# Expert weights split in blocks of 640 columns, their tails multiplied in half modes, squares set apart

## The chip, the cores and the metric

The kernel runs on one core of one Trainium2 chip. The metric is the device time of one execution in microseconds; the time of a kernel is the median of its runs. TensorE (PE in the profile) does the matmuls, VectorE (DVE) and GpSimd (POOL) element-wise work, ScalarE (ACT) copies and activations, SyncE (SP) issues DMAs.

## The reference

Three layers follow each other on 3072 tokens of width 320: a recurrent attention with gates (mLSTM), a mixture of eight experts of which each token goes to one, and a gated layer.

```python
x = attention(q, k, v, gates).reshape(3072, 320)
expert_idx = np.argmax(normed(x) @ normed(expert_emb).T / tau, axis=1)
for e in range(8):
    mask = expert_idx == e
    h = np.maximum(x[mask] @ w1[e], 0.0)             # w1[e]: 320 x 1024
    out[mask] = gate_w[mask, None] * (h @ w2[e])     # w2[e]: 1024 x 320
gate = 1.0 / (1.0 + np.exp(-(out @ w_gate)))         # 320 x 1536
y = (gate * (out @ w_val)) @ w_out                   # 1536 x 320
```

The products are wanted in float32. The kernel makes each from three in half precision: an operand is split in a high half (a copy to float16) and a low half (the operand minus its copy), and high × high, high × low and low × high are added up.

## The kernel before

TensorE goes through three stages: attention up to 131 us, the experts from 131 to 336 us, the gated layer from 336 to 698 us.

**Expert stage.** Tokens are sorted by expert and stand in columns. There are nine runs: runs 0 and 1 are the 512 tokens of expert 0 in two windows of 256 columns, runs 2 to 8 are experts 1 to 7 with windows of 512, 480, 448, 416, 384, 352 and 336 columns. `expert_run(n)` (L1123) does a run in eight steps f, one for each 128 of the 1024 hidden units. In a step `l1_tile` (L1035) makes the hidden values in a PSUM bank `h_ps`, `hidden` (L1136) turns them into `hh` on ScalarE (L1138) and `hl` on VectorE (L1139), and `expert_l2` (L1050) multiplies the hidden values of two steps earlier into the three output banks `y_ps`. The model width 320 is 128 + 128 + 64. For the two slices of 128 each layer has three products per f. For the tail of 64, layer one has a stacked weight tile `w1s` that holds the high half on 64 rows and the low half on the other 64, and layer two has the last 128 columns of `w2h`, high and low half side by side; both then need two full products. So a step has 8 + 8 products of w columns and a run 128. The tails are scaled by 2 to the KT and KU, which is undone later. At the end of a run the tokens of the next are transposed (`transpose_part`, L1021) from rows `xrow` into `xh` and `xl`; a last block that is not full is transposed in as many rows as it has.

**Splits of the weights.** An expert's weights come in four pieces p for each layer, two f's a piece, into raw tiles `w1raw` and `w2raw` with two slots each (p modulo 2), by SyncE. `split_w1` and `split_w2` (L234, L250) split a piece by two ScalarE copies (tail and main part), a small VectorE subtraction for the tail (L216) and a GpSimd subtraction of 512 columns for the main part (L247, L261). `expert_steps` (L1453) sets by hand at which step f of which run a piece is split: odd f's take layer two, even ones layer one, and the load of the piece two further on follows in the same step. In the same steps VectorE works on blocks of the later weights, which arrive as raw 64-bit words: `f64_split` (L1194) is a chain of bit operations on tiles `fa` and `fb` (L1202 to L1219). Each engine runs its instructions in the order in which this code emits them.

**Gated stage.** It has 72 steps t, six groups of 512 tokens by twelve f's. `gated_a` and `gated_b` make gate and value products, in pairs of 64 rows that use both halves of the array; ScalarE takes the sigmoid (L1847) and the copy to `hh` (L1860), and tiny ScalarE copies `seen` (L1817) tell TensorE that the other half's products are done before a bank's rows are swapped. From t = 24 on the loop takes two entries of the list `checks` after each step's `gated_h`; among them are sums of squares of the output weights (`sqw`, L1752) on ScalarE.

## Time and profile before

| | us |
|---|---|
| median of three runs | 704.57 |
| lowest and highest run | 704.1 and 707.03 |
| profiled execution | 709.01 |
| its span | 707.0 |
| attention in it, up to | 131.02 |
| expert runs in it | 131.02 to 336.17 |
| gated stage in it | 336.17 to 697.6 |

The profile shows one execution. TensorE's row of products has the start and the length of each; since products overlap in the array, the distance of two starts, and not the length, is what one costs. The row `PEld` is the loading of weights, which goes beside the products. In the waits an engine's idle time is put down to the instruction that ended it.

### The profile page before, as it was taken

The page shows a single profiled execution, that of the slowest core. Times are in us where ns is not written, and L with a number is a line of the kernel's source. Part 1 is how long each engine was busy: PE and PEld are TensorE (multiplying, and loading weights), DVE is VectorE, ACT ScalarE, POOL GpSimd, SP SyncE. Part 2 cuts the span into 40 slices and gives each one's busy share as a digit, 9 for nine tenths or more (in the row PEclk, how much of TensorE's full clock was granted, in tenths as well). Part 3 has the DMA queues.
Part 4 walks back from the last instruction along what each step waited for, and adds up shares of the span by engine and source line. Part 5 has one row for each costly group of instructions (what it writes and reads, how often), then busy time and mean ns, then how long its engine had stood idle before and what let it go on. Part 6 is the DMA issues. An engine that isn't in the chain of part 4 may idle for free. (4 is left out here: it accounts for less than half of the span.)

```text
span 707.0 us, 17947 instructions
## 1 busy us (share of the span) xinstructions
PE 681.2 (96%) x6955; PEld 428.1 (61%) x6955; DVE 424.8 (60%) x928; ACT 419.7 (59%) x1063; POOL 328.1 (46%) x392
## 2 busy tenths in 40 slices
PE   6999999999999999999999999999999999999994
PEld 6899998885445556666555555545544555555552
DVE  7978888797789999887898873343211122211111
ACT  5887886866966677778665554455455453333332
POOL 8968888543754766674010005343243324324222
PEclk9999999999999999999999999999999999999998
DMA  7655875555445566651223211010010001001001
GB/s 231 212 190 180 276 223 160 150 170 162 138 149 177 162 197 191 197 163 57 57 84 88 63 57 40 1 39 1 2 38 2 1 2 38 2 2 39 1 2 41
DMA packets 39865, 70.47 MB, mean 100 GB/s; under 512 B 4818, under 2 KB 28460, under 8 KB 39772
## 3 DMA queue, kind: packets, MB, share of 16 engines
q1 hardware_dynamic: 36764, 59.61, 28.2%
q0 software_dynamic: 3008, 9.64, 4.2%
q8 instruction: 56, 0.92, 0.6%
q14 instruction: 37, 0.30, 0.2%
HBM read 60.55 MB, written 8.68 MB: 98 GB/s over the span
## 5 line engine op out<-in xcount | busy, mean ns | idle before, releaser
L1848 DVE SCALAR_TENSOR_TENSOR sgm<-v_ps,sgm 128x512 f32<-128x512 f32 (+1 forms) x74 | 49.9, 676 | 201.8 <-ACT sgm L1847 201.8
L1861 POOL TENSOR_TENSOR hl<-sgm,hh 128x512 f16<-128x512 f32 x54 | 62.4, 1159 | 214.2 <-ACT hh L1860 214.1
L1803 PE MATMUL v_ps<-xg,wvh 64*128 64x512 f16 x290 | 108.8, 375 | 3.9 <-ACT seen L1817 3.8
L1803 PE MATMUL g_ps<-xg,wgh 64*128 64x512 f16 x290 | 108.8, 375 | 0.0
L1804 PE MATMUL g_ps<-xg,wgh 64*128 64x512 f16 x290 | 108.6, 375 | 0.0
L1804 PE MATMUL v_ps<-xg,wvh 64*128 64x512 f16 x290 | 108.6, 375 | 0.0
L1805 PE MATMUL g_ps<-xg,wgl 64*128 64x512 f16 x290 | 108.6, 375 | 0.0
L1805 PE MATMUL v_ps<-xg,wvl 64*128 64x512 f16 x290 | 108.6, 375 | 0.0
L1847 ACT ACTIVATE sgm<-g_ps 128x512 f32<-128x512 f32 (+1 forms) x74 | 43.1, 585 | 73.1 <-PE g_ps L1805 70.4
L1884 PE MATMUL o_ps<-wo,hh 64*128 64x320 f16 x560 | 84.9, 296 | 1.4 <-ACT seen L1817 1.4
L1886 PE MATMUL o_ps<-wo,hl 64*128 64x320 f16 x560 | 84.8, 296 | 0.5 <-POOL hl L1861 0.5
L1885 PE MATMUL o_ps<-wo,hh 64*128 64x320 f16 x560 | 84.9, 296 | 0.0
L1860 ACT CAST hh<-sgm 128x512 f16<-128x512 f32 (+1 forms) x74 | 44.8, 606 | 43.2 <-DVE sgm L1848 42.2
L1817 ACT COPY seen<-zeros 1x1 f32<-1x1 f32 x142 | 26.8, 188 | 67.6 <-PE o_ps L1886 37.2
L1055 PE MATMUL y_ps<-hl,w2h 128*128 128x256 f16 (+7 forms) x144 | 46.8, 325 | 1.7 <-DVE hl L1139 1.7
L1043 PE MATMUL h_ps<-xh,w1l 128*128 128x256 f16 (+7 forms) x144 | 47.4, 329 | 0.0
L1042 PE MATMUL h_ps<-xl,w1h 128*128 128x256 f16 (+7 forms) x144 | 47.3, 329 | 0.0
L1041 PE MATMUL h_ps<-xh,w1h 128*128 128x256 f16 (+7 forms) x144 | 47.3, 328 | 0.0
L247 POOL TENSOR_TENSOR w1l<-w1raw,w1h 128x512 bf16<-128x512 f32 x31 | 37.6, 1211 | 20.8 <-ACT w1h L244 19.7
L1054 PE MATMUL y_ps<-hh,w2h 128*128 128x256 f16 (+7 forms) x144 | 46.8, 325 | 0.0
L1056 PE MATMUL y_ps<-hh,w2l 128*128 128x256 f16 (+7 forms) x144 | 46.8, 325 | 0.0
L479 PE MATMUL s_ps<-qk 40*128 40x128 f32 (+1 forms) x384 | 42.1, 300 | 4.5 <-DMA qk<-in_qkt_dram 4.3
(383 smaller groups left out, 1963.1 us busy)
## 6 DMA issues: line engine op xcount, KB each, us to landing
kv<-in_kvo_dram SPq DMA_DIRECT2D x24, 484.0 KB
w2raw<-in_moe_w_dram SPq DMA_DIRECT2D x32, 320.0 KB
w1raw<-in_moe_w_dram SPq DMA_DIRECT2D x32, 256.0 KB
qk<-in_qkt_dram SPq DMA_DIRECT2D x48, 160.0 KB
xs<-x SPq DMA_DIRECT2D x24, 192.0 KB
w1raw<-in_moe_w_dram SPq DMA_DIRECT2D x64, 64.0 KB
raw<-in_moe_w_out_dram SPq DMA_DIRECT2D x12, 320.0 KB
raw<-in_moe_w_gate_dram SPq DMA_DIRECT2D x8, 384.0 KB
```

What stands on the lines that cost most here:

```text
L1041: nc.tensor.matmul(ps, hi[:, kk, fs], h[:, kk], start=(kk == 0), stop=False)
L1042: nc.tensor.matmul(ps, hi[:, kk, fs], l[:, kk], start=False, stop=False)
L1043: nc.tensor.matmul(ps, lo[:, kk, fs], h[:, kk], start=False, stop=False)
L1054: nc.tensor.matmul(ys[d], wh, hh, start=first, stop=False)
L1803: lambda: nc.tensor.matmul(ps, at(wh), h[rows, kk], start=start, stop=False),
L1804: lambda: nc.tensor.matmul(ps, at(wh), l[rows, kk], start=False, stop=False),
L1805: lambda: nc.tensor.matmul(ps, at(wl), h[rows, kk], start=False, stop=stop),
L1848: nc.vector.scalar_tensor_tensor(out=s[:, cs], in0=pv[:, cs], scalar=2.0 ** -KH, in1=s[:, cs], op0=ALU.mult, op1=ALU.mult)
L1861: e.tensor_tensor(out=gl[:, cs], in0=s[:, cs], in1=gh[:, cs], op=ALU.subtract)
L1884: lambda: nc.tensor.matmul(o, gh[rows, ts_], wh[rows], start=begin, stop=False),
L1885: lambda: nc.tensor.matmul(o, gh[rows, ts_], wl[rows], start=False, stop=False),
L1886: lambda: nc.tensor.matmul(o, gl[rows, ts_], wh[rows], start=False, stop=end),
```

## The change

Each piece of expert weights is now one block of 640 columns in `w1h`, `w1l`, `w2h` and `w2l`, split by one ScalarE copy and one GpSimd subtraction over the whole block (`split_piece`); `w1s`, the scales and VectorE's subtractions are gone. The tails become products of half tiles. In layer one (`l1_tails`) the tail weights of two f's lie on the two halves of the rows, and six 64-row products serve both f's, in turn on either half. In layer two (`l2_tails`) the 64 tail columns of two f's go to the two halves of the output rows, six 64-column products for two f's. From run 1 on the layer-one tails of four f's come together ahead of f = 0 and f = 4 and open the banks; the layer-two tails come once ahead of f = 4 (for f's 0 and 1) and else at the end of the run, in the last run partly ahead of its last main products. Run 0 does layer-one tails by two f's and layer-two tails at f = 5 and at its end. `hh` and `hl` get six buffers instead of three, and `h_ps` takes turns in five banks shared with the transposes. Transposes are always 128 wide. The steps in which pieces are split and loaded change, and the gathers of the next run's tokens (`load_x`) come after the GpSimd subtraction of their step. GpSimd's subtractions for experts 2 to 7 wait for the latest closing operation of `f64_split` on VectorE (`holds`, `yields`). In the gated stage from t = 24 on, one entry of `checks` runs ahead of the sigmoid and one after `gated_h`, instead of two after it.

```diff
+    def split_piece(u, k, p, lo=None):
+        t = wraw.pop((u, k, p))
+        hi, low = (z[:, p] for z in ((w1h, w1l), (w2h, w2l))[u - 1])
+        e = lo or nc.gpsimd
+        def sub():
+            ins = e.tensor_tensor(out=low, in0=t, in1=hi, op=ALU.subtract)
+            if k > 1 and e is nc.gpsimd:
+                yields(ins)
+        return [lambda: nc.scalar.copy(hi, t)], [sub]
...
-            m = min(P, s0 + w - j * P)
-            o, xr = tp[:, u * P:u * P + m], xrow[n][0:m, u, kk * P:(kk + 1) * P]
-            nc.tensor.transpose(o, xr, ident[0:m, 0:m])
+            nc.tensor.transpose(tp[:, u * P:(u + 1) * P], xrow[n][:, u, kk * P:(kk + 1) * P], ident)
...
-        nc.tensor.matmul(ps, st[:, fs], h[:, 2], start=False, stop=False)
-        nc.tensor.matmul(ps, st[:, fs], l[:, 2], start=False, stop=True)
...
+    def l1_tails(pss, xt, f):
+        h, l = (z[:, 2] for z in xt)
+        def three(ps, rows):
+            hi, lo = (z[rows, f // 2, 4 * P:] for z in (w1h, w1l))
+            return [
+                lambda: nc.tensor.matmul(ps, hi, h[rows], start=True, stop=False),
+                lambda: nc.tensor.matmul(ps, hi, l[rows], start=False, stop=False),
+                lambda: nc.tensor.matmul(ps, lo, h[rows], start=False, stop=False),
+            ]
+        alternate(*(three(ps, rows) for ps, rows in zip(pss, half_rows)))
...
+    def l2_tails(ys, hs, f):
+        def three(u):
+            rows, (hh, hl) = half_rows[u], hs[u]
+            hi, lo = (z[:, f // 2, u * DM + 2 * P:(u + 1) * DM] for z in (w2h, w2l))
+            o = ys[2][rows]
+            return [
+                lambda: nc.tensor.matmul(o, hi, hh, start=(f == 0), stop=False),
+                lambda: nc.tensor.matmul(o, hi, hl, start=False, stop=False),
+                lambda: nc.tensor.matmul(o, lo, hh, start=False, stop=(f == NF1 - 2)),
+            ]
+        alternate(three(0), three(1))
...
         for f in range(NF1):
-            ps = next_bank((0, 1, 2), "h_ps")[:, 0:w]
-            l1_tile(ps, ws, x, f)
+            if n and f == 4:
+                tails(0)
+            many = 4 if n else 2
+            if f % many == 0:
+                for u in range(f, f + many, 2):
+                    for v in range(2):
+                        pss[u + v] = (tp_ps("h_ps") if n else next_bank((0, 1, 2), "h_ps"))[:, 0:w]
+                    l1_tails([pss[u + v] for v in range(2)], x, u)
+            l1_main(pss[f], x, f)
...
+        if n and not more:
+            tails(2, 4)
         if n:
             l2(NF1 - 2)
             l2(NF1 - 1)
+        tails(*range(NF1 - len(h), NF1, 2))
...
-                if f % 2:
-                    refill(f, 1, k + f // 4, (f // 2 + 2) % 4)
-                elif f or k > 1:
-                    refill(f, 0, k + (f > 0), (f // 2 + 3) % 4)
+                if f in (0, 1, 3):
+                    refill(f, 1, k, (f + 3) // 2, nc.vector if k == 1 and f == 0 else None)
+                elif f == 5:
+                    refill(f, 1, k + 1, 0)
                 else:
-                    refill(f, 1, 1, 1, nc.vector)
+                    refill(f, 0, k + 1, f // 2 - (f < 7))
...
+            if t >= 2 * NF2:
+                check(t)
         weave(rest[0])
         weave(rest[1])
         s = gated_b(t)
...
-        for _ in range(1 + (t >= 2 * NF2)):
-            if t > 1 and t not in xsteps and checks and (len(checks) > 15 or not (ready or todo)):
-                checks.pop(0)()
+        check(t)
```

On TensorE, where run 4 (448 columns) hands over to run 5 (416 columns), the kernel before had the last layer-two products and then the first step's layer one, with its tail at the end:

```order
2990 L1058 MATMUL y_ps<-hh,w2h 128x448
2991 L1059 LDWEIGHTS w2h
2992 L1059 MATMUL y_ps<-hl,w2h 128x448
2993 L1041 LDWEIGHTS w1h
2994 L1041 MATMUL h_ps<-xh,w1h 128x416
...
3006 L1044 MATMUL h_ps<-xh,w1s 128x416
3007 L1045 LDWEIGHTS w1s
3008 L1045 MATMUL h_ps<-xl,w1s 128x416
```

The changed kernel has there the end of 18 layer-two tail products (64 output rows), then twelve layer-one tail products for four f's, and only then the first full product (L1042):

```order
3135 L1079 MATMUL y_ps<-hh,w2l 64x448
3136 L1079 LDWEIGHTS w2l
3137 L1079 MATMUL y_ps<-hh,w2l 64x448
3138 L1060 LDWEIGHTS w1h
3139 L1060 MATMUL h_ps<-xh,w1h 128x416
3140 L1060 LDWEIGHTS w1h
3141 L1060 MATMUL h_ps<-xh,w1h 128x416
...
3161 L1062 MATMUL h_ps<-xh,w1l 128x416
3162 L1042 LDWEIGHTS w1h
3163 L1042 MATMUL h_ps<-xh,w1h 128x416
```

The tails moved out of the steps into two places of a run, and the array changes between full, column halves and row halves there.

On VectorE, at the start of the same run, the kernel before has a small subtraction of the tails between the low halves of the hidden values:

```order
514 L1139 SCALAR_TENSOR_TENSOR hl<-h_ps,hh 128x416
515 L216 SCALAR_TENSOR_TENSOR w1s<-w1raw,w1s 64x256
516 L1139 SCALAR_TENSOR_TENSOR hl<-h_ps,hh 128x416
517 L216 SCALAR_TENSOR_TENSOR w2h<-w2raw,w2h 128x2x64
518 L1139 SCALAR_TENSOR_TENSOR hl<-h_ps,hh 128x416
519 L216 SCALAR_TENSOR_TENSOR w1s<-w1raw,w1s 64x256
520 L1202 TENSOR_SCALAR fa<-raw_4161 128x384
521 L1205 TENSOR_SCALAR fb<-raw_4161 128x384
522 L1208 SCALAR_TENSOR_TENSOR fb<-raw_4161,fb 128x384
523 L1139 SCALAR_TENSOR_TENSOR hl<-h_ps,hh 128x416
```

The changed kernel has there:

```order
480 L1168 SCALAR_TENSOR_TENSOR hl<-h_ps,hh 128x416 x3
481 L1248 TENSOR_SCALAR fa<-raw_4161 128x384
482 L1251 TENSOR_SCALAR fb<-raw_4161 128x384
483 L1254 SCALAR_TENSOR_TENSOR fb<-raw_4161,fb 128x384
484 L1168 SCALAR_TENSOR_TENSOR hl<-h_ps,hh 128x416
```

The subtractions of the tails have left VectorE's queue; the chain on the 64-bit words stands where it stood.

On ScalarE, in the gated stage where the squares of the output weights begin, the kernel before has two squares between a step's copy to `hh` and the next `seen` copies:

```order
708 L1847 ACTIVATE sgm<-g_ps 128x512
709 L1860 CAST hh<-sgm 128x512
710 L1752 ACTIVATE sqw,wsum<-wo 128x640 x2
711 L1817 COPY seen<-zeros 1x1 x2
712 L1847 ACTIVATE sgm<-g_ps 128x512
```

The changed kernel has one on either side of sigmoid and copy:

```order
645 L1863 COPY seen<-zeros 1x1 x2
646 L1799 ACTIVATE sqw,wsum<-wo 128x640
647 L1893 ACTIVATE sgm<-g_ps 128x512
648 L1906 CAST hh<-sgm 128x512
649 L1799 ACTIVATE sqw,wsum<-wo 128x640
650 L1863 COPY seen<-zeros 1x1 x2
```

One of the two squares moved from ahead of the `seen` copies to behind them, ahead of the next sigmoid.

## Rows read from the trace of the kernel before

**Rows 1.** The page: busy time, share of the span and instructions of each engine.

```profile
PE 681.2 (96%) x6955; PEld 428.1 (61%) x6955; DVE 424.8 (60%) x928; ACT 419.7 (59%) x1063; POOL 328.1 (46%) x392
```

**Rows 2.** Run 5 as a stretch: length, busy PE, PEld, DVE, ACT, POOL; clock, DMA.

```profile
251.92:275.45 23.53, 23.53 (x138) 13.53 (x137) 22.94 (x36) 16.82 (x45) 15.30 (x15) 1.00 0.61 179
```

**Rows 3.** Waits of PE in the expert stage: total, times, longest in us.

```profile
PE y_ps L1055 <- DVE hl L1139: 1.7, 2, 1.1
PE sp_ps L1010 <- DVE xl L216: 0.6, 1, 0.6
```

**Rows 4.** Waits of PE in the gated stage, the largest.

```profile
PE v_ps L1803 <- ACT seen L1817: 3.8, 8, 1.9
```

**Rows 5.** Timeline of PE, run 5's first step: start, length, instruction.

```profile
252.97 0.34 PE L1044 MATMUL h_ps<-xh,w1s 128*128 128x416 f16 x1
253.15 0.34 PE L1045 MATMUL h_ps<-xl,w1s 128*128 128x416 f16 x1
```

**Rows 6.** Timeline of PE: transposes for run 5 and for run 6.

```profile
246.98 1.97 PE L1028 MATMUL tp_m<-ident,xrow 128*128 128x128 f32 x12
...
271.66 1.15 PE L1028 MATMUL tp_m<-ident,xrow 128*128 128x128 f32 x9
```

**Rows 7.** Timeline of PE: pairs on row halves in the gated stage.

```profile
500.65 0.30 PE L1884 MATMUL o_ps<-wo,hh 64*128 64x320 f16 x2
500.79 0.30 PE L1885 MATMUL o_ps<-wo,hh 64*128 64x320 f16 x2
```

**Rows 8.** Attention: timeline of PE around L529; weight loads of L529, min/median/max ns.

```profile
53.86 0.66 PE L529 MATMUL u_ps<-vw,kv 128*64 128x41 f32 x16
54.45 1.16 PE L479 MATMUL s_ps<-qk 40*128 40x128 f32 x16
...
L529 PEld LDWEIGHTS u_ps<-vw,kv x320: 112/126/138, 16.7 to 109.4; 128*64 128x64 f32 x100, 128*40 128x40 f32 x60
```

**Rows 9.** Timeline of PE at two changes between full and half tiles.

```profile
288.29 0.33 PE L1059 MATMUL y_ps<-hl,w2h 128*128 128x384 f16 x1
288.55 0.24 PE L1325 MATMUL pn_ps<-ident,y 24*128 24x24 f32 x1
288.72 0.34 PE L1041 MATMUL h_ps<-xh,w1h 128*128 128x384 f16 x1
...
335.93 0.31 PE L1059 MATMUL y_ps<-hl,w2h 128*128 128x336 f16 x1
336.17 0.39 PE L1803 MATMUL g_ps<-xg,wth 64*128 64x512 f16 x1
```

**Rows 10.** Groups by line, 165 to 345 us: busy us, mean ns; idle before.

```profile
L216 DVE SCALAR_TENSOR_TENSOR w1s<-w1raw,w1s 64x256 f16<-64x256 f32 x25 | 18.7, 747 | 2.2 <-ACT w1s L221 1.5
...
L247 POOL TENSOR_TENSOR w1l<-w1raw,w1h 128x512 bf16<-128x512 f32 x25 | 30.3, 1213 | 16.1 <-ACT w1h L244 16.0
```

**Rows 11.** Timeline of VectorE in run 5.

```profile
258.39 1.91 DVE L216 SCALAR_TENSOR_TENSOR w1s<-w1raw,w1s 64x256 f16<-64x256 f32 x1
...
260.61 3.05 DVE L1205 TENSOR_SCALAR fb<-raw 128x384 int32<-128x384 int32 x1
...
264.17 0.58 DVE L1139 SCALAR_TENSOR_TENSOR hl<-h_ps,hh 128x416 f16<-128x416 f32 x1
```

**Rows 12.** Timeline of two gated steps; the first product of a step is `wth`.

```profile
553.76 0.38 PE L1803 MATMUL g_ps<-xg,wth 64*128 64x512 f16 x1
...
555.95 0.74 ACT L1752 ACTIVATE sqw<-wo 128x640 bf16<-128x640 f16 x1
...
556.91 0.39 PE L1803 MATMUL v_ps<-xg,wvh 64*128 64x512 f16 x1 [0.23 <-ACT seen L1817]
...
559.03 0.38 PE L1803 MATMUL g_ps<-xg,wth 64*128 64x512 f16 x1
...
563.90 0.38 PE L1803 MATMUL g_ps<-xg,wth 64*128 64x512 f16 x1
```

**Rows 13.** The page's costliest groups: sigmoids; busy us, mean ns; idle before.

```profile
L1847 ACT ACTIVATE sgm<-g_ps 128x512 f32<-128x512 f32 (+1 forms) x74 | 43.1, 585 | 73.1 <-PE g_ps L1805 70.4
```

More of the change, by code (lines that the diff above doesn't have):

```diff
@@ L63 @@
     KX, KW, KH, KD = 19, 10, 13, 11
-    KS, KT, KU = 15, 4, 8
+    KS = 15
+    NH_ = 6
     SLO, SHI = 2.0 ** -14, 3.99
@@ L199, in load_w1, with holds, yields @@
     def load_w1(k, p):
[L201 to L202 removed]
+        t = w1r[:, p % 2, 0:PW]
         w = w1[expert(k)][0][:, p * 2 * P:(p + 1) * 2 * P]
[L204 removed]
+        nc.sync.dma_start(
+            out=t[:, 0:4 * P].rearrange("p (k f) -> p k f", k=2), in_=w[0:2 * P].rearrange("(k p) f -> p k f", p=P)
+        )
         for u in range(2):
[L206 to L207 removed]
+            nc.sync.dma_start(out=t[u * RM:(u + 1) * RM, 4 * P:], in_=w[2 * P:DM, u * P:(u + 1) * P])
+        wraw[1, k, p] = t
     def load_w2(k, p):
[L210 removed]
+        t = w2r[:, p % 2, 0:PW]
         w = w2[expert(k)][0][p * 2 * P:(p + 1) * 2 * P]
[L212 removed]
+        nc.sync.dma_start(
+            out=t.rearrange("p (k d) -> p k d", k=2), in_=w.rearrange("(k p) d -> p k d", p=P)
+        )
         wraw[2, k, p] = t
     def scaled_sub(dst, x, k, y):
[L216 removed]
+        return nc.vector.scalar_tensor_tensor(
             out=dst, in0=x, scalar=2.0 ** k, in1=y, op0=ALU.mult, op1=ALU.subtract
         )
+    sync = mybir.DependencyInfo(mybir.DependencyClass.Sync, mybir.DependencyReason.DATA)
+    port = []
+    def holds(op):
+        port[:] = [op()]
+    def yields(ins):
+        if port:
+            tc.add_manual_dep(ins.ins, port[0].ins.name, sync, reason="VectorE goes first")
+        return ins
     def scaled_copy(dst, x, k):
@@ new lines, with alternate @@
+    half_rows = [slice(u * RM, (u + 1) * RM) for u in range(2)]
+    def alternate(*chains):
+        for ops in zip(*chains):
+            for op in ops:
+                op()
+    def l1_tails(pss, xt, f):
[8 more added lines that the diff above has]
+        alternate(*(three(ps, rows) for ps, rows in zip(pss, half_rows)))
@@ L1056, in expert_l2 @@
             nc.tensor.matmul(ys[d], wl, hh, start=False, stop=last)
-        wr = w2h[:, f, 2 * P:]
-        nc.tensor.matmul(ys[2], wr, hh, start=first, stop=False)
-        nc.tensor.matmul(ys[2], wr, hl, start=False, stop=last)
     def expert_out(n, ys, g=None):
@@ L1126, in expert_run @@
         x = tuple(t[:, :, 0:w] for t in xt[n])
-        ws = (w1h, w1l, w1s)
         ys, gb = [], []
@@ L1141, in hidden, with tails @@
             )
+        def tails(*fs):
+            for f in fs:
+                l2_tails(ys, [h.pop(f + u) for u in range(2)], f)
+        pss = {}
         for f in range(NF1):
-            ps = next_bank((0, 1, 2), "h_ps")[:, 0:w]
-            l1_tile(ps, ws, x, f)
+            if n and f == 4:
[7 more added lines that the diff above has]
+            l1_main(pss[f], x, f)
             if n == 0:
                 yield
-            hidden(ps, f)
+            hidden(pss.pop(f), f)
             if f >= 2:
                 l2(f - 2)
+            if n == 0 and f == 5:
+                tails(0, 2)
             yield
@@ L1507, in expert_steps @@
                 next(run_)
-            if more and f < len(blocks(n + 1)):
-                load_x(n + 1, (f,))
             prepare(f)
@@ L1516, in expert_steps @@
             weave(*rest[f])
+            if more and f < len(blocks(n + 1)):
+                load_x(n + 1, (f,))
             weave(ends[f])
@@ L1957, with check @@
     late = []
+    def check(t):
+        if t > 1 and t not in xsteps and checks and (len(checks) > 15 or not (ready or todo)):
+            checks.pop(0)()
     for t in range(NG * NF2):
```

114 lines of the change are left out of this document (40 added, 74 removed).

## The prediction

> **What bounds the kernel now.** I read the page's busy shares first: TensorE is busy for 96% of the span [rows 1], so time can only come out of TensorE's own work or out of its few waits. I then cut the span into the nine expert runs and the gated stage. A middle run shows the rule for runs 3 to 8: run 5 lasts 23.53 us and TensorE is busy for 23.53 us of it at the full clock, while VectorE is busy for 22.94 us as well [rows 2]. So TensorE is the bound, and VectorE stands just behind it. The table of TensorE's waits in the expert stage holds little: 1.7 us for two low halves of hidden values (both in run 1) and 0.6 us once for `xl` [rows 3]. In the gated stage the one steady wait is for the small ScalarE copies `seen`, 3.8 us in eight places, of which 1.9 us is a single one [rows 4].
>
> The profiled execution took 709.01 us with a span of 707.0 us, so about 2 us lie around the span; the median of the runs is 704.57 us, 4.4 us below that execution. I make the sum as differences against the profiled span and take it off the median.
>
> **Tails in half modes: the gain.** Before, the third slice of the model width (64 of 320 columns) costs two full matmuls of each eight in both layers. At run 5's start the two products with `w1s` begin 0.18 us apart, as a full product does [rows 5]. Run 5 has 128 products; its 23.53 us [rows 2] less about 1.0 us for nine transposes (1.15 with the last one's run-out [rows 6]) makes 0.176 us each at 416 columns, 0.4235 ns a column. The seven runs 2 to 8 have 512+480+448+416+384+352+336 = 2928 columns, so one product in each of them costs 1.24 us together. After, the tail of a pair of f's is six half products on each half, run side by side: six slots a pair and layer, thus 12 + 12 slots a run for tails instead of 16 + 16. Eight slots a run go: 8 × 1.24 = **-9.9 us**, and in the two 256-column runs 8 × 0.108 × 2 = **-1.7 us**.
>
> This needs pairs to run side by side. For row halves the trace shows it: in the gated stage two 64-row products of 320 columns start together and the next pair starts 0.14 us later, the price of one [rows 7]. For column halves (layer two) the nearest rows are the attention's state updates: 16 products on 64-column halves follow each other in 0.59 us, though each has its own weight load of 126 ns in the median, 2.0 us of loads in all [rows 8]. Loads and products of the two halves therefore overlap there, and I price a column pair as one slot. Its other end is two slots, since those products have only 41 columns (second rival).
>
> A rule speaks against it: the Trainium skill ("TensorE: Matmul & The Clock Gate", Part 3, The mechanism) says that a weight load overlaps a running product only where the row group differs, and both column halves use all rows. By the same page's load formula (columns over 1.2, LDWEIGHTS) 24 bare loads of 64 columns would cost an estimated 1.3 us a run, 11.5 us in all, and the sum would come out at 706.6 us, a case counted with the second rival. Against the rule stands [rows 8], where the loads would need 2.0 us by themselves, and [rows 2], where 13.53 us of full-row loads vanish inside a run in which TensorE never pauses.
>
> **Mode switches: the price.** Going from full to half tiles drains the array. From the last full product of the expert stage to the first 64-row product 0.24 us pass instead of 0.14, so 0.10; around the one 24-row transpose 0.26 us instead of 0.16 going in, and 0.17 us for a product worth a few hundredths coming out [rows 9]. I take 0.12 each, with ends of 0.10 and 0.17. By the order, a run from run 1 on enters column halves, goes to row halves and back to full twice: 6 switches; run 8 has one more of its own, and run 0, which does its tails two f's at a time, about 11. That is 43 in runs 2 to 8, 6 in run 1 and 11 in run 0: 60 × 0.12 = **+7.2 us** (6.0 to 10.2).
>
> **Transposes.** All are 128 wide now. Twelve with a 32-row form among them took 1.97 us, nine full ones 1.15 [rows 6]; twelve full ones cost at most 1.15 × 12/9 = 1.53, so 0.45 is saved in each of the two runs with 64 or 32 leftover rows; in three other runs the leftover grows by 32 to 48 rows, +0.2 together. **-0.7 us.**
>
> **Splits of weights.** They lie off TensorE's path, under its products. VectorE loses the subtractions of both tails, 18.7 us over the expert stage for layer one's alone [rows 10], and as many for layer two; GpSimd's blocks grow from 512 to 640 columns, at most 1.213 × 640/512 = 1.5 us each [rows 10]. What VectorE loses counts only where it is late. In run 1 those are the 1.7 us of [rows 3], behind two `w1s` subtractions; in run 2 the 0.6 us behind `xl`. **-2.3 us.** On the other side the distance from hidden(f) to the layer-two products that use it falls from 32 slots to 24: at 416 columns from 5.6 to 4.2 us. How close that is shows in run 5, where a `w1s` subtraction of 1.91 us and then an `fb` operation of 3.05 us stand in front of one `hl` that ends at 264.75 [rows 11], about when its product is due. Without the subtraction that `hl` could come 1.9 us sooner, and its product wants it 1.4 us sooner: even. GpSimd now waits for VectorE's last operation of a piece; behind its subtraction stand the gathers of x for the next run, now moved after it, which have most of a run left, so that is hidden, and SyncE's reload of the raw block, which waited for a subtraction before too. Some reloads have three steps of f where they had four, 8.5 us at 416 columns; no row here prices a landing, so its lateness goes to the third rival. For waits that open here and there I add **+0.8 us** (ends 0 and 8; near the lower one, since the handover of [rows 11] comes out even).
>
> **Squares apart.** From t = 24 on twelve steps of the gated stage hold two squares of 0.74 us in a row on ScalarE [rows 12], and the `seen` copies come behind them. One such step took 5.27 us (553.76 to 559.03) where the next took 4.87, and its wait for `seen` was 0.23 us [rows 12]. With one square ahead of the sigmoid the copies come 0.74 us sooner. That square needs cover: ScalarE idles for 73.1 us over 74 sigmoids waiting for `g_ps`, 1.0 us each [rows 13], so it fits. I take 0.23 for each of twelve steps, **-2.8 us**; the ends are 1.9 (the waits of [rows 4] without the long one) and 4.8 (0.40 in every step).
>
> **The sum.** -9.9 - 1.7 + 7.2 - 0.7 - 2.3 - 2.8 + 0.8 = -9.4 us, and 704.57 - 9.4 = 695.1 us.
>
> **Rivals.**
> First, on the gaining side: switches at 0.10 (-1.2), squares at 4.8 (-2.0), no new waits (-0.8): 691 us. Below 690 only if several of these bounds are short; chance 0.05.
>
> Second, on the other side: column pairs run one after the other, in the layer-two tails alone. Then each run pays 24 slots for them instead of 12, 12 × (1.24 + 2 × 0.108) = 17.5 us more: 712.6 us. It turns to a loss from 54% of this price on (9.4 of 17.5). For it speaks that no row shows two column halves fed by long different streams; against it the 0.59 us of [rows 8]. Chance 0.09, most of it slower, some at no change where only part of the overlap fails.
>
> Third, the expert stage is bound by its feeders. GpSimd's longer subtractions wait for VectorE, a reload comes late, a copy that waits for it blocks ScalarE in front of a hidden value, and TensorE waits with fewer slots in hand. For it speak VectorE at 22.94 of 23.53 us in run 5 and the 3.05 us `fb`; against it the 18.7 us, and layer two's share, that VectorE no longer has to do. At 1 us in each of five to eight runs it eats 5 to 8 us: 700 to 703 us. Chance 0.14. The Trainium skill ("SBUF — State Buffer", the table entry on the shared port pair) says that VectorE and GpSimd hold a shared port for a whole instruction; by that rule a longer subtraction stretches each such stall; [rows 11] agrees as far as one `fb` took 3.05 us.
>
> **How the numbers follow.** The forecast itself, 690 to 700 us, has 0.72. Half a per cent, 3.5 us, is about what a measurement of this kernel can tell from no change. Faster than 701.05: 0.72 + 0.05 + not quite half of the third rival = 0.83. Within: the rest of that rival and a little of the second, 0.10. Slower: 0.07. The range 689.5 to 703 holds forecast and third rival and leaves out the column rival.
>
> **What would show it.** In the profile after, run 5 should last about 22.9 us: 120 slots (21.2), six switches (0.7) and nine transposes (1.0). Layer-two tail products should start in twos, one slot apart, and the first product after each change of mode 0.10 to 0.17 late. The waits of [rows 3] should be gone, and steps from t = 24 on near 4.9 us. I am wrong on the column pairs if their starts are one slot apart singly; wrong on the feeders if TensorE's waits in the expert stage, 2.3 us now, exceed some 4 us; wrong on the squares if the gated stage is not 2 to 5 us shorter.

## The result and the profile after

The changed kernel is slower: 709.93 us (706.98 to 711.96, 14 runs) against 705.22 us for the kernel before, a ratio over all runs of 1.0061 with a 95% interval of 1.0047 to 1.0075 (the quotient of the two medians is 1.0067). The forecast was 695.1 us, 689.5 to 703. On a second chip the same two kernels stood at 712.59 and 711.10 us, 1.0011 (0.9994 to 1.0027): there no difference can be told. So it is slower by 0 to 0.7% depending on the chip, and on neither the 1.3% faster that was forecast. Each experiment below is given as a ratio to the kernel before on the same chip, and to be compared with 1.0011 to 1.0061; that comparison is across chips.

The page of the changed kernel, busy times of the engines; the row answers to [rows 1]:

```profile
PE 677.8 (96%) x7099; PEld 428.9 (60%) x7099; DVE 405.6 (57%) x869; ACT 407.7 (57%) x994; POOL 337.0 (48%) x387
```

TensorE, VectorE and ScalarE all have less to do than before, GpSimd a little more, and the span is 2.1 us longer. Most of the gain went into waits. Cut by stages, the expert stage of before and after, and below them runs 4 and 5 of the changed kernel, in the columns of [rows 2]:

```profile
131.02:336.17 205.15, 202.56 (x1285) 124.69 (x1285) 176.13 (x324) 148.99 (x397) 118.21 (x107) 0.99 0.53 159
```

```profile
131.09:346.19 215.10, 201.92 (x1428) 115.17 (x1427) 156.48 (x262) 138.33 (x334) 127.72 (x105) 0.98 0.48 143
...
227.31:256.48 29.17, 26.85 (x159) 13.22 (x158) 24.24 (x30) 17.11 (x39) 17.96 (x15) 0.94 0.59 172
256.48:280.80 24.32, 23.19 (x157) 12.41 (x155) 19.32 (x24) 15.71 (x37) 17.25 (x14) 1.00 0.56 164
```

The stage grew from 205.15 to 215.10 us. Run 5 took 24.32 us where the forecast wanted 22.9 and the kernel before had 23.53 [rows 2]; VectorE is busy for 19.32 us of it and no longer 22.94, and still TensorE waits for it. The gated stage went the other way, from 370.8 us (336.17 to the span's end) to 362.9.

Part of the 10 us is the clock. TensorE's granted clock has two levels, 1.2 and 2.4 GHz (0.50 and 1.00 in these rows). Two stretches of the changed kernel's stage are at the lower one, and in the kernel before one (last row):

```profile
131.09:136.59 5.50, 5.50 (x39) 3.41 (x39) 2.42 (x10) 3.27 (x9) 2.08 (x3) 0.50 0.36 115
252.64:256.05 3.41, 3.41 (x19) 1.36 (x19) 2.38 (x5) 0.00 (x0) 0.46 (x1) 0.50 0.26 71
```

```profile
131.53:134.94 3.41, 3.41 (x25) 2.51 (x24) 1.49 (x8) 2.66 (x9) 1.30 (x2) 0.50 0.57 173
```

So 8.9 us of the stage against 3.4 ran at the lower level. A slot takes twice as long there (0.37 us instead of 0.19 at 448 columns), so half of such a stretch is lost, by this estimate. The first of them began ahead of the stage, at 129.76 us, and across the traces of the changed kernel and of the edits below to its expert and gated stages, which all have the same attention stage, 0 to 5.5 us of the expert stage's start are at the lower level. The stage's length in one trace can therefore be off by almost 3 us for a reason that is not the edit's; what an edit is worth is better read from the times of the runs.

TensorE's waits in the changed kernel's expert stage, the larger ones; the 2.3 us of [rows 3] stand here as 11.6:

```profile
PE y_ps L1090 <- DVE hl L1168: 8.9, 10, 2.0
PE tp_m L1028 <- DVE hl L1168: 1.1, 1, 1.1
PE sp_ps L1009 <- DVE hl L1168: 1.0, 1, 1.0
PE h_ps L1060 <- DVE hl L1168: 0.6, 1, 0.6
```

All ten waits of the first row lie at ends of runs: five on the hidden values of f = 5, one on f = 6 and four on f = 7. The timeline of TensorE at the worst, the end of run 4 (448 columns):

```profile
249.59 0.35 PE L1089 MATMUL y_ps<-hh,w2h 128*128 128x448 f16 x1
251.98 0.35 PE L1090 MATMUL y_ps<-hl,w2h 128*128 128x448 f16 x1 [2.04 <-DVE hl L1168]
...
253.33 0.58 PE L1077 MATMUL y_ps<-hh,w2h 128*64 128x448 f16 x2
253.70 0.58 PE L1078 MATMUL y_ps<-hl,w2h 128*64 128x448 f16 x2
...
256.19 0.35 PE L1079 MATMUL y_ps<-hh,w2l 128*64 128x448 f16 x2
```

The wait costs 2.04 us, and then the tail products follow each other at 0.37 us instead of 0.19: the clock is at its lower level until about 256, 1.7 us more.

The switches and pairs, timeline of TensorE in the middle of run 5, with one row of its weight loads (PEld):

```profile
263.80 0.34 PE L1091 MATMUL y_ps<-hh,w2l 128*128 128x416 f16 x1
264.07 0.37 PE L1077 MATMUL y_ps<-hh,w2h 128*64 128x416 f16 x2
264.10 0.11 PEld L1078 LDWEIGHTS <-w2h 128*64 128x64 f16 x2
264.27 0.34 PE L1078 MATMUL y_ps<-hl,w2h 128*64 128x416 f16 x2
264.45 0.34 PE L1079 MATMUL y_ps<-hh,w2l 128*64 128x416 f16 x2
264.72 0.35 PE L1060 MATMUL h_ps<-xh,w1h 64*128 64x416 f16 x2
...
265.61 0.34 PE L1062 MATMUL h_ps<-xh,w1l 64*128 64x416 f16 x2
265.88 0.35 PE L1042 MATMUL h_ps<-xh,w1h 128*128 128x416 f16 x1
```

Column halves (128*64) and row halves (64*128) both come in twos (x2), a pair every 0.18 us, as [rows 5] has it for single products. A change of mode takes 0.27 us from start to start, 0.09 more than a slot.

Last, what VectorE did in run 5 before one of those waits, beside GpSimd:

```profile
269.03 1.41 POOL L253 TENSOR_TENSOR w2l<-w2raw,w2h 128x640 bf16<-128x640 f32 x1
...
269.26 3.62 DVE L1248 TENSOR_SCALAR fa<-raw 128x384 int32<-128x384 int32 x1
...
270.39 1.40 POOL L253 TENSOR_TENSOR w1l<-w1raw,w1h 128x640 bf16<-128x640 f32 x1
...
271.75 0.91 POOL L1269 TENSOR_TENSOR wgl<-fa,wgh 128x384 f16<-128x384 f32 x1
...
273.67 0.57 DVE L1168 SCALAR_TENSOR_TENSOR hl<-h_ps,hh 128x416 f16<-128x416 f32 x1
...
274.30 0.34 PE L1090 MATMUL y_ps<-hl,w2h 128*128 128x416 f16 x1 [0.68 <-DVE hl L1168]
```

One bit operation `fa`, 0.35 us at its shortest in this trace, lasts 3.62 us, while three GpSimd operations run in a row, and ends 0.2 us after the last of them. `hl` stands behind it.

### The profile page after: what moved, and what is told of

It is laid out like the page before. It is cut to its first block, busy times and chain, and to the rows that moved or that the text cites. A ratio compares the mean times of both kernels' runs of the same rounds, so it can differ in the third digit from the quotient of the medians.

```text
span 709.1 us, 18068 instructions
## 1 busy us (share of the span) xinstructions
PE 677.8 (96%) x7099; PEld 428.9 (60%) x7099; DVE 405.6 (57%) x869; ACT 407.7 (57%) x994; POOL 337.0 (48%) x387
## 5 line engine op out<-in xcount | busy, mean ns | idle before, releaser
L1932 PE MATMUL o_ps<-wo,hl 64*128 64x320 f16 x560 | 86.3, 296 | 0.8 <-POOL hl L1907 0.8
L1930 PE MATMUL o_ps<-wo,hh 64*128 64x320 f16 x560 | 86.3, 296 | 0.0
L1931 PE MATMUL o_ps<-wo,hh 64*128 64x320 f16 x560 | 86.3, 296 | 0.0
L253 POOL TENSOR_TENSOR w2l<-w2raw,w2h 128x640 bf16<-128x640 f32 x28 | 40.3, 1441 | 53.1 <-ACT w2h L257 36.5
L1168 DVE SCALAR_TENSOR_TENSOR hl<-h_ps,hh 128x256 f16<-128x256 f32 (+7 forms) x72 | 39.6, 551 | 37.1 <-ACT hh L1167 37.1
L1090 PE MATMUL y_ps<-hl,w2h 128*128 128x256 f16 (+7 forms) x144 | 46.9, 326 | 9.2 <-DVE hl L1168 8.9
L253 POOL TENSOR_TENSOR w1l<-w1raw,w1h 128x640 bf16<-128x640 f32 x31 | 43.5, 1403 | 21.2 <-ACT w1h L257 14.9
L1042 PE MATMUL h_ps<-xh,w1h 128*128 128x256 f16 (+7 forms) x144 | 47.8, 332 | 0.0
```

The source lines that it names most:

```text
L253: ins = e.tensor_tensor(out=low, in0=t, in1=hi, op=ALU.subtract)
L1042: nc.tensor.matmul(ps, hi[:, kk], h[:, kk], start=False, stop=False)
L1930: lambda: nc.tensor.matmul(o, gh[rows, ts_], wh[rows], start=begin, stop=False),
L1931: lambda: nc.tensor.matmul(o, gh[rows, ts_], wl[rows], start=False, stop=False),
L1932: lambda: nc.tensor.matmul(o, gl[rows, ts_], wh[rows], start=False, stop=end),
```

## The experiments

**Which part makes the values late.** Theories: the gathers, moved behind subtractions, block ScalarE (G); GpSimd's longer blocks stretch VectorE's operations (V); TensorE leaves too few slots between a value and its use (S). Four kernels on one chip, each the changed kernel with one edit.

Gathers ahead again:

```diff
+            if more and f < len(blocks(n + 1)):
+                load_x(n + 1, (f,))
             prepare(f)
...
             weave(*rest[f])
-            if more and f < len(blocks(n + 1)):
-                load_x(n + 1, (f,))
```

> The changed kernel with one edit: the gathers of the next run's tokens are issued before GpSimd's subtraction of their step, as in the kernel before. Theory G (the gathers come late behind subtractions that wait for VectorE; ScalarE, which scales the gathered rows ahead of the next hidden value, stands still 15.8 us for them, and hidden values come late): ScalarE's waits for xrow fall under 3 us, TensorE's waits for hl in the expert stage fall from 8.9 us to about half, the time falls by 4 to 6 us, to about 705 us. Theory V (VectorE's bit operations are stretched by GpSimd's longer blocks): xrow's waits fall too, but TensorE's waits for hl stay above 7 us, and the time falls by less than 1.5 us. Theory S (24 slots instead of 32 between a hidden value and its use are too few whatever feeds them): as V.

Measured: 1.0009 (0.9988 to 1.0030). ScalarE's 15.8 us of waiting for `xrow` are gone, and TensorE waits as before:

```profile
PE y_ps L1090 <- DVE hl L1168: 9.1, 10, 2.1
```

The gathers' move fell as a cause: a long wait, on an engine that has the time.

No hold of GpSimd:

```diff
-            if k > 1 and e is nc.gpsimd:
-                yields(ins)
```

> The changed kernel with one edit: GpSimd's subtractions no longer wait for the closing operation of VectorE's chain on the 64-bit words. Theory G: subtractions and the gathers behind them come earlier, ScalarE waits less for xrow (under 10 us of 15.8), the time falls by 1 to 3 us. Theory V: the wait kept GpSimd's blocks off the chain, without it the bit operations grow longer still (mean above 1.0 us against 0.997 now), the time rises by 1 to 3 us. Theory S: no change beyond 1 us.

Measured: 1.0017 (1.0001 to 1.0032); TensorE's waits for `hl` at L1088 (L1090 above) 6.1 us instead of 8.9, the expert stage 212.63 us instead of 215.10, with 5.3 us of it at the lower clock instead of 8.9. Against 1.0011 to 1.0061 that is no change that can be told. The hold neither helps nor hurts by more than some 2 us.

Layer-two tails ahead of the last two main parts:

```diff
-        if n and not more:
+        if n:
             tails(2, 4)
```

> The changed kernel with one edit: in every run from run 1 on the layer-two tails of f = 2 to 5 (six slots each pair of pairs) come ahead of the last two main parts of layer two, as the last run has it, which gives the last two hidden values 6 slots more (0.9 to 1.3 us) and costs two more switches in seven runs, 14 x 0.09 = 1.3 us. Theory S: the waits at the ends of runs, some 8 us with the low clock that follows one of them, shrink to under 2 us, and the time falls by 4 to 6 us. Theories G and V: the values are late by up to 2 us, six slots cover about half of it, the time falls by 1 to 3 us.

Measured: 0.9975 (0.9962 to 0.9988), 709.50 us, some 3 us less than the first two kernels (712.96 and 712.38 us on this chip), at an estimated 1.3 us more for switches. The waits for `hl` at `y_ps` fell from 8.9 to 6.1 us. The expert stage took 208.97 us, 6.1 us less than in the changed kernel, but this trace has a granted clock of 1.00 over the whole stage, also at its start, which the edit does not touch; so part of the 6.1 is not the edit's. Slots at the end of a run help, by 3 us and not by the 4 to 6 of S: the size is that of G and V, and waits stay.

Subtractions on VectorE:

```diff
-        e = lo or nc.gpsimd
+        e = lo or (nc.vector if k > 1 else nc.gpsimd)
```

> The changed kernel with one edit: the low halves of the weights of experts 2 to 7 are made by VectorE instead of GpSimd (0.83 us for a block of 640 columns by the one such row in the trace, 1.41 on GpSimd). Theory V: with GpSimd's blocks gone, the five bit operations of VectorE's chain fall from a mean of 997 ns to 320 to 560 ns, which gives back some 30 us of VectorE against some 40 us for the 49 subtractions; TensorE's waits for hl fall under 5 us and the time falls by 3 to 6 us. Theory S: VectorE is as full as before, the waits stay at 8 to 12 us, the time stays within 2 us. Theory G: the gathers find GpSimd free, ScalarE's waits for xrow fall under 5 us and the time falls by 4 to 6 us.

Measured: 0.9931 (0.9907 to 0.9954), 706.41 us, some 6 us less than the first two kernels; the expert stage 208.56 us, with 10.2 us of it at the lower clock. VectorE's groups in the changed kernel (first) and in this one (second): total us and mean ns.

```profile
L1248 DVE TENSOR_SCALAR fa<-raw 128x384 int32<-128x384 int32 x13 | 18.2, 1398 | 0.0
L1254 DVE SCALAR_TENSOR_TENSOR fb<-raw,fb 128x384 int32<-128x384 int32 x13 | 15.2, 1168 | 0.4
L1262 DVE SCALAR_TENSOR_TENSOR fb<-raw,fb 128x384 int32<-128x384 int32 x13 | 12.2, 935 | 0.0
L1251 DVE TENSOR_SCALAR fb<-raw 128x384 int32<-128x384 int32 x13 | 9.6, 741 | 0.0
L1265 DVE SCALAR_TENSOR_TENSOR fa<-fb,fa 128x384 int32<-128x384 int32 x13 | 9.6, 741 | 1.4
```

```profile
L253 DVE TENSOR_TENSOR w2l<-w2raw,w2h 128x640 bf16<-128x640 f32 x25 | 20.6, 823 | 8.6 <-ACT w2h L257 8.3
L253 DVE TENSOR_TENSOR w1l<-w1raw,w1h 128x640 bf16<-128x640 f32 x24 | 19.6, 818 | 4.2 <-ACT w1h L257 3.8 <-DMA raw<-in_moe_w_val_dram 0.5
L1248 DVE TENSOR_SCALAR fa<-raw 128x384 int32<-128x384 int32 x13 | 8.3, 641 | 0.0
L1254 DVE SCALAR_TENSOR_TENSOR fb<-raw,fb 128x384 int32<-128x384 int32 x13 | 7.7, 590 | 0.4
L1265 DVE SCALAR_TENSOR_TENSOR fa<-fb,fa 128x384 int32<-128x384 int32 x13 | 7.3, 558 | 0.5
L1262 DVE SCALAR_TENSOR_TENSOR fb<-raw,fb 128x384 int32<-128x384 int32 x13 | 7.1, 549 | 0.0
L1251 DVE TENSOR_SCALAR fb<-raw 128x384 int32<-128x384 int32 x13 | 6.0, 465 | 0.0
```

The five groups of the chain fell from 64.8 to 36.4 us, none above 1.31 us, and VectorE took over 40 us of subtractions: it is busier than in the changed kernel (161 us of the stage against 156) and the values come sooner (waits for `hl` at `y_ps` 3.2 us). So it is not VectorE's load that makes them late but stalls of up to 3.6 us at one place. Both V and S have something.

**The changed kernel, its squares, and the two edits together**, on a second chip. The changed kernel as it is:

> The changed kernel once more, beside the others of this call, so that they can be compared on one chip. All theories: slower than the kernel before by about 0.6%, as on the first chip, with the gated stage beginning near 346 us.

Measured: 1.0011 (0.9994 to 1.0027), the gated stage from 346.05 us: the same expert stage (214.88 us) and a smaller loss.

Squares two in a row again:

```diff
             gated_l2h(t - 2, 0)
-            if t >= 2 * NF2:
-                check(t)
...
-        check(t)
+        for _ in range(1 + (t >= 2 * NF2)):
+            check(t)
```

> The changed kernel with the squares of the gated stage two in a row again. By the forecast's term it is 2.8 us slower than the changed kernel (1.9 to 4.8). Rival: the wait for the seen copies was covered in most steps, and the time is within 1 us of the changed kernel.

Measured: 716.69 us, 1.0076 (1.0049 to 1.0103), 4.1 us above the changed kernel on this chip. The term was right in kind: 4.1 for 2.8, inside its ends of 1.9 and 4.8, and by the two intervals not to be told from 2.8.

No hold and tails ahead (the diffs of the second and third kernel together):

> The changed kernel without the wait of GpSimd for VectorE and with the layer-two tails ahead of the last two main parts in every run. If hold (about 3 us of the expert stage) and slots at the end of a run (about 7 us with the low clock behind one wait) are separate prices, the gated stage begins near 337 us and the time is 6 to 9 us below the changed kernel. If they are the same lateness seen twice, it begins near 339 us, 5 to 6 us below.

Measured: 0.9984 (0.9968 to 1.0000), the gated stage from 340.27 us: no more than tails ahead alone. The hold is no price of its own.

Subtractions on VectorE and tails ahead (the diffs of the third and fourth kernel together):

> The changed kernel with the subtractions of experts 2 to 7 on VectorE and the layer-two tails ahead of the last two main parts. If the stretching of VectorE's operations by GpSimd's blocks is the cause of the late values, little waiting is left (under 3 us) and the gated stage begins at 333 to 335 us, before the 336.17 of the kernel before; the time is 10 to 13 us below the changed kernel and below the kernel before by 0.8 to 1.2%. If VectorE's load alone is the cause, waits stay above 5 us and it begins near 338 us.

Measured: 703.54 us, 0.9893 (0.9872 to 0.9914), faster than both kernels; the expert stage 204.15 us, its waits for `hl`:

```profile
PE y_ps L1090 <- DVE hl L1168: 1.8, 3, 1.2
PE sp_ps L1009 <- DVE hl L1168: 1.8, 1, 1.8
PE h_ps L1060 <- DVE hl L1168: 0.6, 1, 0.6
```

By the runs, this is 9 us below the changed kernel on the same chip: the two prices, some 6 and 3 us alone, add up. (The stage is 11.0 us shorter, but with 3.4 us at the lower clock instead of 8.9.)

**Blocks or bunches, and slots by a longer lag.** Each GpSimd subtraction in two halves:

```diff
-            ins = e.tensor_tensor(out=low, in0=t, in1=hi, op=ALU.subtract)
-            if k > 1 and e is nc.gpsimd:
-                yields(ins)
+            for c in (slice(0, PW // 2), slice(PW // 2, PW)):
+                ins = e.tensor_tensor(out=low[:, c], in0=t[:, c], in1=hi[:, c], op=ALU.subtract)
+                if k > 1 and e is nc.gpsimd:
+                    yields(ins)
```

> The changed kernel with each GpSimd subtraction of 640 columns cut into two of 320 (about 0.9 us each by the rows of 256, 512 and 640 columns, so GpSimd is busy longer in all: 1.8 us a piece). Theory B (a VectorE operation that meets a block waits for the block's whole length, so the length of a block is what makes hidden values late): VectorE's longest bit operations fall from 3.6 us to under 2.2 us, TensorE's waits for hl fall under 7 us, the time falls by 2 to 4 us. Theory T (what counts is the total time that GpSimd works beside VectorE): total grows by a quarter, the bit operations' mean stays at 1.0 us or above, and the time is the same or up to 3 us longer.

Measured: 1.0009 (0.9989 to 1.0029), the expert stage 215.17 us. The timeline of VectorE and GpSimd in run 6:

```profile
292.99 1.54 POOL L254 TENSOR_TENSOR w2l<-w2raw,w2h 128x320 bf16<-128x320 f32 x2
293.18 3.94 DVE L1249 TENSOR_SCALAR fa<-raw 128x384 int32<-128x384 int32 x1
294.49 1.53 POOL L254 TENSOR_TENSOR w1l<-w1raw,w1h 128x320 bf16<-128x320 f32 x2
295.99 0.90 POOL L1270 TENSOR_TENSOR wtl<-fa,wth 128x384 f16<-128x384 f32 x1
```

VectorE does not get in between the halves: `fa` waits out five GpSimd operations in a row, 3.94 us. It is the unbroken row of GpSimd's operations that counts here, not the length of one. Theory B fell, and total time (T) is nearer; the two halves take 1.54 us, not the 1.8 expected.

Layer two three steps behind:

```diff
             if n and f == 4:
-                tails(0)
+                l2_tails(ys, [h[u] for u in range(2)], 0)
...
-            if f >= 2:
-                l2(f - 2)
+            lag = 3 if n else 2
+            if f >= lag:
+                l2(f - lag)
+            if n and f == 4:
+                h.pop(0), h.pop(1)
...
+        if n:
+            l2(NF1 - 3)
         if n and not more:
             tails(2, 4)
```

> The changed kernel with layer two's main part three steps behind layer one from run 1 on instead of two. TensorE does the same products with the same switches; a hidden value has six slots more before its use, 0.9 to 1.3 us. Theory S (too few slots): waits for hl fall from 9 us to under 3, the time falls by 5 to 8 us. Theory V (stretched VectorE operations): the values are late by 0.4 to 2.2 us, so six slots cover most of the short waits and half of the long ones, waits of 4 to 6 us stay, the time falls by 3 to 4 us.

Measured: 1.0066 (1.0044 to 1.0088), a loss and no gain; the expert stage 218.80 us, with 12.2 us of it at the lower clock. Its three largest waits for `hl`:

```profile
PE tp_m L1028 <- DVE hl L1168: 2.9, 3, 2.2
PE h_ps L1060 <- DVE hl L1168: 2.7, 3, 1.9
PE y_ps L1090 <- DVE hl L1168: 1.8, 4, 0.9
```

At `y_ps` the wait fell from 8.9 to 1.8 us as S says, and TensorE ran on into the next thing that the same `hl` holds: the bank of a transpose or of the next layer-one tails, which `hl` has still to read. Both theories missed this. All waits of TensorE in the stage rose from 12.8 to 15.3 us: a distance that is lengthened in one place only moved the wait.

The same lag with the subtractions on VectorE:

> Lag of three steps and the subtractions of experts 2 to 7 on VectorE, with no extra switches. If slots and stretching are separate prices, waits for hl fall under 2 us from run 2 on, the gated stage begins at 332 to 334 us and the kernel is 1.2 to 1.6% faster than the kernel before. If they are the same lateness seen twice, it stands where the variant with tails ahead and VectorE stands, 1.1% faster.

Measured: 0.9941 (0.9919 to 0.9964), the gated stage from 335.59 us, behind the variant with tails ahead (0.9893, on another chip).

The kernel before with the squares apart (the reverse of the squares' diff):

> The kernel before with one part of the change alone: the squares of the gated stage one ahead of the sigmoid and one after. If squares are worth in the kernel before what they are worth in the changed one (4.1 us in medians there), it is 4 us faster than the kernel before (0.994). By the forecast's term it is 2.8 us faster (0.996). Rival: the gain hung on the changed kernel's schedule, 1.000.

Measured: 0.9925 (0.9898 to 0.9951), 5.3 us (3.5 to 7.3) faster than the kernel before: the squares are a gain without the rest of the change, and faster than the whole of it.

**Slots or splits, on the kernel before.** Two of sixteen products a step left out, splits as they are:

```diff
-        nc.tensor.matmul(ps, st[:, fs], h[:, 2], start=False, stop=False)
-        nc.tensor.matmul(ps, st[:, fs], l[:, 2], start=False, stop=True)
+        nc.tensor.matmul(ps, st[:, fs], h[:, 2], start=False, stop=True)
...
-        nc.tensor.matmul(ys[2], wr, hh, start=first, stop=False)
-        nc.tensor.matmul(ys[2], wr, hl, start=False, stop=last)
+        nc.tensor.matmul(ys[2], wr, hh, start=first, stop=last)
```

> The kernel before without two of its sixteen products a step (the tails' products with the low halves xl and hl are left out, so the output lacks those small terms). Its splits stay as they are; between a hidden value and its use stand 28 slots instead of 32, and a run has 112 slots, fewer than the 120 of the changed kernel. TensorE loses 16 products a run, 16 x (1.24 + 0.216) = 23.3 us. Theory S (TensorE now outruns what feeds it, whatever the splits): its waits in the expert stage rise from 3 us to 10 us or more, and the time falls by 10 to 16 us. Theory V (GpSimd's subtractions beside VectorE's chain): waits stay under 6 us, the time falls by 20 to 23 us.

Measured: 0.9887 (0.9865 to 0.9909), 8 us less for 23.3 us of products; the expert stage 196.33 us, 8.8 less than 205.15, with 3.4 us at the lower clock in both. TensorE's waits, the two largest:

```profile
PE y_ps L1054 <- DVE hl L1137: 9.0, 12, 2.2
PE sp_ps L1010 <- DVE xl L216: 2.2, 1, 2.2
```

With the kernel before's own splits the same waits open as soon as slots are taken away; 14 of 23 us come back. S holds.

The tails' subtractions on GpSimd, slots as they are:

```diff
-        pre, sub = tail_sub(w1s[lower, fs], r[lower], KT, w1s[lower, fs], k == 0 and lo is None)
+        pre, sub = tail_sub(w1s[lower, fs], r[lower], KT, w1s[lower, fs], lo is None)
...
-        pre, sub = tail_sub(w2h[:, f, DM:], r, KU, w2h[:, f, 2 * P:DM], k == 0 and lo is None)
+        pre, sub = tail_sub(w2h[:, f, DM:], r, KU, w2h[:, f, 2 * P:DM], lo is None)
```

> The kernel before with the tails' low halves made by GpSimd for all experts, not by VectorE (with one more small ScalarE copy a piece to scale the raw tail). Slots and products stay as they are. Theory V: with all subtractions on GpSimd the bit operations are met by GpSimd oftener (more than 10 of 70 over 1.5 us against 4), TensorE's waits rise from 3 us to 8 us or more, the time rises by 4 to 8 us. Theory S: VectorE has 35 us less to do, 32 slots are enough, waits stay at 1 to 4 us, the time is the same.

Measured: 1.0321 (1.0292 to 1.0350), much worse than either theory had it, and by another way: only one bit operation is above 1.5 us. The expert stage took 228.90 us, 23.7 us of it at the lower clock. One of ScalarE's waits, from 166 us on, and TensorE's largest:

```profile
ACT w1s L221 <- DMA w1raw<-in_moe_w_dram: 11.1, 3, 4.0
```

```profile
PE y_ps L1054 <- ACT hh L1138: 8.1, 4, 3.2
```

A copy on ScalarE waits for a reload, and `hh` stands behind it; that the reloads are late because raw tiles come free late is the likely reading. The edit also gives ScalarE one more small copy a piece, which was not tested apart. This run says that GpSimd has little room, and nothing on V.

**What the answers are worth.** Subtractions on VectorE, tails and gathers ahead (the diffs of the first, third and fourth kernel together):

> The changed kernel with subtractions on VectorE, tails ahead of the last main parts and the gathers ahead as in the kernel before. Without gathers ahead it stood 1.1% below the kernel before. If GpSimd is free anyway the gathers come no earlier: 0.989 again. If the first run's waits (1.2 us for hl, 0.2 for xrow) hang on them: 0.987.

Measured: 0.9914 (0.9892 to 0.9937): the gathers bring nothing here either.

Layer one's subtractions on VectorE, layer two's on GpSimd without the hold, tails and gathers ahead:

```diff
-        e = lo or nc.gpsimd
+        e = lo or (nc.vector if k > 1 and u == 1 else nc.gpsimd)
...
-            if k > 1 and e is nc.gpsimd:
-                yields(ins)
```

> The changed kernel with layer one's subtractions on VectorE and layer two's on GpSimd without the hold, gathers and tails ahead. If any GpSimd subtraction beside the chain costs alike, the expert stage stands half way between the variant with all on GpSimd (209 us with tails ahead) and all on VectorE (204 us): about 206.5 us, ratio about 0.993. If only two blocks in a row hurt, which layer two alone seldom has: about 204 us, ratio 0.989.

Measured: 0.9900 (0.9873 to 0.9926), the expert stage 205.07 us, waits for `hl` at `y_ps` 3.7 us. Eleven bit operations are above 1.5 us, none above 2.13. Half of the subtractions off GpSimd are enough, in a trace with no lower clock in the stage; that it is the long rows of GpSimd operations that were broken up is likely and not shown by this run alone.

The kernel before with squares apart and the main subtractions on VectorE (in both split functions `e` as in the fourth kernel):

> The kernel before with the squares apart and the main parts' subtractions of experts 2 to 7 on VectorE; products and slots as before. Squares alone gave a ratio of 0.9925. If 32 slots cover what GpSimd's blocks make late, nothing more comes of it: 0.991 to 0.995, with 2 to 4 us of waits in the expert stage. If the blocks cost something there too, the stage shortens by 2 us or more and the ratio is under 0.990.

Measured: 0.9942 (0.9923 to 0.9961), no better than squares alone; the expert stage 206.18 us. Where the slots are as before, GpSimd's blocks cost nothing that can be told.

The variant with VectorE and tails ahead, on the same chip:

> The changed kernel with subtractions on VectorE and tails ahead, again, for the same chip as e17. Without waits the half modes are worth 11.6 us of slots less 6.7 us of switches, about 5 us or 0.7%: ratio 0.985 to 0.990, below e17 by 0.3 to 0.7%. If what feeds TensorE bounds the stage in both, they are equal within 0.2%.

Measured: 704.62 us, 0.9899 (0.9875 to 0.9923), 2.6 us below the kernel of the last paragraph. The intervals just touch. The stage was 207.10 us here, 204.15 us the other time and 206.18 us in the other kernel, with 8.9, 3.4 and 3.8 us at the lower clock; with half of that taken off, an estimate, they stand at 202.6, 202.4 and 204.3 us. That the half modes bring some 2 us once the feeders are helped is likely from both and not beyond doubt.

## Why the prediction was wrong

**What was right.** Column pairs and row pairs take one slot, 0.18 us at 416 columns. Switches cost 0.09, not 0.12, so 60 of them 5.4 us instead of 7.2. The transposes for run 4 went from 1.99 us to 1.31, 0.68 for one run where 0.45 was taken. The eight slots a run are gone. By these terms alone the expert stage should have come down by 11.6 - 5.4 + 0.7 = 6.9 us, to some 198 us. The rule of the Trainium skill ("TensorE: Matmul & The Clock Gate", Part 3, The mechanism) that loads overlap only between different row groups does not hold here: the pairs at 264.07 to 264.45 share all rows and run a slot apart, and the loads of the second pair (264.10) go beside the products of the first.

**What failed** is one step, "for waits that open here and there I add +0.8 us", with the -2.3 us beside it. Instead of 198 the stage took 215.1 us, 17 us more. The waits of TensorE in it sum up to 12.8 us by the table (11.6 of them in the four rows above) against 2.5 before, 10 of the 17. Counted from start to start over all products of the two traces, so with the little that is lost around each wait (2.20 us at 251.98 where the table has 2.04), the waits make up 12.7 of the 17; the lower clock is 2.6, of it 1.7 after the wait at 251.98 and 0.9 at the stage's start; small delays of single products are some 1.4. The -2.3 did not come either: in run 1 a wait of 1.04 us at 160.72 and one of 0.42 at 164.51 stand where there were 1.7, and `sp_ps` waits 1.0 us instead of 0.6.

The failing thought was that the handover of [rows 11] "comes out even": 1.9 us gained by the subtraction that VectorE loses, 1.4 us lost in slots. The gain did not arrive, because the 1.91 us of that `w1s` subtraction was for the most part delay and not work: a GpSimd subtraction ran beside it from 258.84 to 260.00. Shortest, median and longest of its kind in the kernel before's expert stage, in ns:

```profile
L216 DVE SCALAR_TENSOR_TENSOR w1s<-w1raw,w1s x29: 421/422/1908, 139.7 to 320.3; 64x256 f16<-64x256 f32 x29
```

Both layers' tail subtractions took 39.1 us there; with each at the shortest of its kind they would take 20.6, so some 18.5 us were delay (an estimate). The operations left, the delay came down on others: in the kernel before the five groups of the chain took 52.9 us, in the changed one 64.8, though the chain is the same, and of 65 such operations 15 instead of 4 lasted over 1.5 us. That it is the same delay that moved is read from these sums; no run tests it alone. Several of the long ones come where the last hidden values of a run are due, as `fa` in run 5 above. The loss in slots arrived in full. The lower end of the bound, chosen as the nearer, was the wrong end, and the upper one, 8 us, was too low; the third rival had the place and the sign and was priced at half. Its evidence stood in [rows 2]: VectorE busy for 22.94 of 23.53 us says that TensorE's 100% was no proof that products alone set the pace.

**What is shown and what is not.** Shown: slots taken from the kernel before bring the waits up with no other change (14 of 23 us come back); by the times of the runs the subtractions off GpSimd are worth some 6 us in the changed kernel, the tails ahead some 3, both 9; off GpSimd in the kernel before they take nothing. So the waits hang on two things together, fewer slots and GpSimd's operations beside VectorE's. Not the cause: the gathers, the hold, the length of one block. Not separated: whether GpSimd's rows hurt more in the changed kernel by its order of pieces, by the 640 columns, or only because the tails' subtractions no longer take a part of the delay. Open as well: why the lower clock comes in some traces and not in others.

**Squares.** The sign and the mechanism held: steps of 4.87 us in a row at 550 us (545.14, 550.01, 554.88), where with squares in pairs one of them takes 5.27. The term was 2.8; the runs give 4.1 in the changed kernel and 5.3 (3.5 to 7.3) in the kernel before. In the first two traces the gated stage is 7.9 us shorter, but 4.1 of that are two single steps (from 526.76 and 584.63 us, 6.94 and 6.85 us long) that take 4.87 in the changed kernel here and 6.36 and 6.86 in its trace on the second chip, so they are not the squares'; all other steps from t = 24 on give 3.0 us together, close to the term. It is the one part of the change that was shown to pay by itself.

## What to carry to other kernels

An engine at 100% is the bound only as far as those that feed it have time in hand: before taking work from it, ask how late each handover is in front of it, and test it by leaving a little work out, which needs one run. Count slots between a value and its use as a price of their own, in every resource that the value holds, PSUM banks included. Look at rows of GpSimd operations beside VectorE as one block, and before counting an operation's removal as a gain, compare its longest time with its median: what is delay does not leave with it. And look at the granted clock before comparing a stage between two traces.

## What was not expected of the hardware

A VectorE operation of 0.35 us took 3.94 us while five GpSimd operations followed each other, and halving these did not let it in. After a wait of 2.04 us TensorE ran at the lower level of its clock for some 3.4 us; but with squares in pairs, where the expert stage is the same, a wait of 2.12 us at the same place (250.60) was followed by no such stretch, and the longest wait of the kernel with layer one's subtractions on VectorE, 2.41 us, by none either. A change between full, row-half and column-half tiles cost 0.09 to 0.10 us in all three directions.
